# Attention keys in 16 KB runs and 2 MB loads, a gather moved between transposes, the store from ScalarE

## The chip, the cores and the metric

The kernel runs on one core of a Trainium2 chip. The metric is the device time of one execution in microseconds (us); lower is better. The core has TensorE (PE, its weight loads PEld), VectorE (DVE), ScalarE (ACT), GpSimd (POOL) and SyncE (SP), which work side by side and wait for each other through semaphores. Transfers between the device memory and the on-chip memory are issued by SP or ACT and are carried out by 16 DMA engines. TensorE writes its results to PSUM, from where VectorE and ScalarE read them.

## The reference

One decoding step: eight batches, one query token each. `x` is normalised, attention runs over the last 1,024 of 4,096 cached positions, with 32 query heads on 8 kv heads, and its result is multiplied by a gate from a small feed-forward net. All inputs are bf16.

```python
def A(x, k_cache, v_cache, wq, wo):          # x (8, 1, 512), caches (8, 8, 4096, 128)
    W = 1024
    q = (x @ wq).reshape(8, 1, 32, 128).transpose(0, 2, 1, 3)
    k = repeat(k_cache[:, :, -W:, :], 4, axis=1)
    v = repeat(v_cache[:, :, -W:, :], 4, axis=1)
    p = softmax(q @ k^T * 128 ** -0.5)
    return (p @ v).transpose(0, 2, 1, 3).reshape(8, 1, 4096) @ wo

def B(x, w_gate, w_up, w_down):
    return (gelu(x @ w_gate) * (x @ w_up)) @ w_down

xn = layernorm(x)
out = x + A(xn, ...) * silu(B(xn, ...))
```

The window of keys is 16.8 MB, that of values as much. wq and wo are 4.2 MB each, w_gate, w_up and w_down 1.8 MB each. (Below, MB in the sizes of loads stands for 1,024 x 1,024 bytes: a set is 1 MB.)

## The kernel before, in words

**Sets.** The attention is cut into 16 sets: set s is kv head s // 2 with batches 0 to 3 (s even) or 4 to 7 (s odd). `load_set` (L105) brings a set's keys or values as one DMA of 1 MB: partition 4p + g holds, for batch g of the set, the 32 positions 32p to 32p + 31, which lie together in the device memory, 8 KB. Rows of neighbouring batches lie 8 MB apart there. The tiles come from the pool `ring` with 9 buffers (L68), keys and values together. The weights come through `big` (L69), 5 buffers of 2 MB, used in turn: three loads of wq (1, 1 and 2 MB), w_gate, w_up, w_down, and two tiles for wo.

**One set's way.** All of it is done with four batches at once:

- `transpose_quarter` (L400), four times a set: four TensorE transposes of 128x128 f32 (two bf16 in each) by the identity `identf` into a PSUM tile `kT_ps` (four buffers), which VectorE (even quarter, L414) or ScalarE (odd, L416) copies into `kT` as 128x1024 bf16.
- `scores` (L420): eight matmuls with the queries (L425) into `sc`; VectorE adds the mask of the batches and takes each row's maximum (L433).
- `maxima` (L441): two f32 matmuls (L444) bring the row maxima together in `m_ps`; VectorE makes the bias of the exponential from them (L449).
- `exponentials` (L455): ScalarE's Exp with its sum (L458). `turn` (L466): VectorE transposes the result (L468).
- `value_half` (L474), twice: eight matmuls each with the values (L479); after the second, ScalarE copies the sum to `blk` (L486).
- `gather` (L490), once a head, for its two sets: eight matmuls (L496) into `m_ps`, the same PSUM tile that `maxima` uses; VectorE divides (L502 to L507) and turns the result into `oR` (L512).

**The order of work** is written out by hand, in steps t of half a set, and each engine works through its own list in that order:

```python
for t in range(2 * NS + LV + 3):          # NS = 16, LV = 5: t = 0 to 39
    s, i = divmod(t, 2)
    # i == 0: exponentials(s-2); fetch K(s)
    # transpose_quarter(s, 2*i), transpose_quarter(s, 2*i + 1); two hidden_steps
    # i == 0: turn(s-2), scores(s-1)
    # i == 1: gather((s-4)//2) for even s >= 4, then maxima(s-1)
    # value_half of set (t - 5) // 2; t = 6, 7: down(0), down(1); t = 8: fold(), gate()
```

So set s is transposed in steps 2s and 2s+1, scored in 2s+2, its maxima are taken in 2s+3, its exponentials in 2s+4, its values in 2s+5 and 2s+6. The last gather, that of head 7, is in step 37; nothing is left for the two steps behind it. `hidden_steps` are the eight operations of the feed-forward net's middle; `down`, `fold` and `gate` are its end.

**The queues.** SP issues every load, in the order in which the loop fetches: wq in three loads (L99), w_gate, w_up, K0, K1, K2, w_down, then V0, K3, V1, K4 and so on to V12, K15, V13, V14, V15, and last wo (L128) in eight pieces, 1 MB, five of 512 KB, 384 KB and 128 KB. A load waits for its buffer to be free, and every load behind it on SP waits too. ScalarE issues one load, x (L90). After the loop, 128 matmuls (L587) multiply `oR` by wo, VectorE applies the gate (L598) and adds x (L599), and SP stores the 8 KB result (L600).

Of the kernel before, what the change touches and what calls it, by code (L numbers as in the profile page):

```python
# [11 lines left out]
BF16 = mybir.dt.bfloat16  # L12
FP32 = mybir.dt.float32
# [4 lines left out]
def kernel(  # L18
# [13 lines left out]
    nc = tc.nc  # L32

    B, Sq, D = A_x.shape
    Hkv, Sk, Dh = A_k_cache.shape[1], A_k_cache.shape[2], A_k_cache.shape[3]
# [3 lines left out]
    win0 = Sk - W  # L39
# [4 lines left out]
    P = nc.NUM_PARTITIONS  # L44
# [2 lines left out]

    G = 4  # L50
    NB = B // G
    NS = Hkv * NB
    KP = P // G
    NCH = W // KP
    NC = G * rep
    SET = NCH * Dh
    QT = 4
    CP = NCH // 2
    QP = CP // QT
# [5 lines left out]


    lead = ctx.enter_context(tc.tile_pool(name="lead", bufs=1))
    ring = ctx.enter_context(tc.tile_pool(name="ring", bufs=9))  # L68
    big = ctx.enter_context(tc.tile_pool(name="big", bufs=5))  # L69
    kT_pool = ctx.enter_context(tc.tile_pool(name="kT_pool", bufs=2))  # L70
    p_pool = ctx.enter_context(tc.tile_pool(name="p_pool", bufs=2))
# [1 line left out]
    small = ctx.enter_context(tc.tile_pool(name="small", bufs=3))  # L73
# [31 lines left out]
    def load_set(cache, s):  # L105
        h, b0 = s // NB, (s % NB) * G
        t = slot()
        nc.sync.dma_start(
            out=t,
            in_=cache[b0 : b0 + G, h, win0:Sk, :].rearrange(  # L110
                "g (p c) d -> p g (c d)", p=KP
            ),
        )
        return t.rearrange("p (c d) -> p c d", c=NCH)

    HB = 2 * SET // (rep * D)
    wo_tiles = {}
# [279 lines left out]

    K, V, kT, sc, P_, pT, blk = {}, {}, {}, {}, {}, {}, {}

    def transpose_quarter(s, i):  # L400
        ps = ps_kT.tile([P, QP, P], FP32, name="kT_ps")
        for c in range(QP):
            nc.tensor.transpose(  # L403
                ps[:, c, :],
                K[s][:, 2 * (i * QP + c) : 2 * (i * QP + c) + 2, :]
                .rearrange("p c d -> p (c d)").bitcast(FP32),
                identf,
            )
        if i == 0:
            kT[s] = kT_pool.tile([P, CP, P, 2], BF16, name="kT")  # L410
        out = kT[s][:, i * QP : (i + 1) * QP].rearrange("p c k e -> p (c k e)")
        in_ = ps.rearrange("p c k -> p (c k)").bitcast(BF16)
        if i % 2 == 0:
            nc.vector.tensor_copy(out=out, in_=in_)  # L414
        else:
            nc.scalar.activation(out=out, in_=in_, func=ACT.Copy)  # L416

    top = {}

    def scores(s):  # L420
        ps = ps_sc.tile([P, CP, 32], FP32, name="sc")
        t = kT.pop(s)
        for e in range(2):
            for R in range(NR):
                nc.tensor.matmul(  # L425
                    ps[32 * R : 32 * R + 32],
                    qT[:, e, s].rearrange("p c b j -> p (c b j)"),
                    t[:, :, 32 * R : 32 * R + 32, e],
                    start=(e == 0), stop=(e == 1), skip_group_check=True,
                )  # L430
        sc[s] = small.tile([P, CP * 32], FP32, name="sc_sb", bufs=2)
        top[s] = small.tile([P, 1], FP32, name="top")
        nc.vector.tensor_tensor_reduce(  # L433
            out=sc[s], in0=ps.rearrange("p c k -> p (c k)"),
            in1=own.rearrange("p c b g -> p (c b g)"),
            op0=ALU.add, op1=ALU.max, scale=1.0, scalar=NEG, accum_out=top[s],
        )
# [3 lines left out]
    def maxima(s):  # L441

        ps = m_top
        nc.tensor.matmul(  # L444
            ps, top.pop(s).to_broadcast([P, P]), identf, start=True, stop=True
        )
        scr = small.tile([P, P], FP32, name="scr", bufs=1)
        bias = small.tile([P, 1], FP32, name="bias")
        nc.vector.tensor_tensor_reduce(  # L449
            out=scr, in0=ps, in1=same.rearrange("p x n -> p (x n)"),  # L450
            op0=ALU.add, op1=ALU.min, scale=-scale, scalar=-NEG, accum_out=bias,
        )
        biases[s] = bias

    def exponentials(s):  # L455
        blk[s] = small.tile([P, 2, Dh + 1], FP32, name="blk", bufs=4)
        P_[s] = p_pool.tile([P, CP * 32], BF16, name="p")
        nc.scalar.activation(  # L458
            out=P_[s], in_=sc.pop(s), func=ACT.Exp, scale=scale, bias=biases.pop(s),
            accum_out=blk[s][:, 0, Dh : Dh + 1],  # L460
        )
        nc.gpsimd.tensor_copy(  # L462
            out=blk[s][:, 1, Dh : Dh + 1], in_=blk[s][:, 0, Dh : Dh + 1]
        )

    def turn(s):  # L466
        pT[s] = p_pool.tile([P, CP, 32], BF16, name="pT")
        nc.vector.transpose(  # L468
            out=pT[s].rearrange("p c k -> p (c k)"), in_=P_.pop(s)
        )  # L470
# [3 lines left out]
    def value_half(s, i):  # L474
        if i == 0:
            o_ps[s] = ps_o.tile([P, 2, Dh], FP32, name="o_ps")
        for c in range(i * CP // 2, (i + 1) * CP // 2):
            q = c % NR
            nc.tensor.matmul(  # L479
                o_ps[s][32 * q : 32 * q + 32].rearrange("p c d -> p (c d)"),  # L480
                pT[s][:, c, :],
                V[s][:, 2 * c : 2 * c + 2, :].rearrange("p c d -> p (c d)"),
                start=(c < NR), stop=(c >= CP - NR), skip_group_check=True,
            )
        if i == 1:
            nc.scalar.activation(out=blk[s][:, :, 0:Dh], in_=o_ps.pop(s), func=ACT.Copy)  # L486
            pT.pop(s)
            V.pop(s)

    def gather(h):  # L490

        ps = m_out
        for b in range(NB):
            t = blk.pop(h * NB + b)
            for c in range(2):
                nc.tensor.matmul(  # L496
                    ps, sums[:, c, b].rearrange("p j b f -> p (j b f)"), t[:, c, :],
                    start=(b == 0 and c == 0), stop=(b == NB - 1 and c == 1),
                )

        rec = small.tile([P, 1], FP32, name="rec")
        nc.vector.tensor_scalar(  # L502
            out=rec, in0=ps[:, Dh : Dh + 1], scalar1=0.5, scalar2=None, op0=ALU.max
        )
        nc.vector.reciprocal(out=rec, in_=rec)
        o = small.tile([P, rep, Dh // rep], BF16, name="o")
        nc.vector.tensor_scalar(  # L507
            out=o, in0=ps[:, 0:Dh].rearrange("p (i r) -> p r i", r=rep),
            scalar1=rec, scalar2=None, op0=ALU.mult,
        )  # L510

        nc.vector.transpose(  # L512
            out=oR[:, h].rearrange("p r b -> p (r b)"),
            in_=o.rearrange("p r i -> p (r i)"),
        )


    AHEAD = 3
    down_tiles = []
    seq = []  # L520
    for s in range(AHEAD):
        seq.append(("K", s))
    seq.append(("D", 0))
    for s in range(NS):
        seq.append(("V", s))
        if s + AHEAD < NS:
            seq.append(("K", s + AHEAD))
    pending = list(seq)

    def fetch(kind, s):  # L530
        while True:
            k, i = pending.pop(0)
            if k == "K":
                K[i] = load_set(A_k_cache, i)
            elif k == "V":
                V[i] = load_set(A_v_cache, i)
            else:
                down_tiles.append(load_rows(B_w_down, 0, NFC, NFC, "wd"))
            if (k, i) == (kind, s):
                return  # L540


    LV = 2 * (AHEAD - 1) + 1
    for t in range(2 * NS + LV + 3):
        s, i = divmod(t, 2)
        if i == 0 and 0 <= s - 2 < NS:
            exponentials(s - 2)
        if s < NS:
            if i == 0:
                fetch("K", s)  # L550
            transpose_quarter(s, 2 * i)
            transpose_quarter(s, 2 * i + 1)
        for _ in range(2):
            if hidden_steps:
                hidden_steps.pop(0)()
        if i == 0 and 0 <= s - 2 < NS:
            turn(s - 2)
        if i == 0 and 0 <= s - 1 < NS:
            scores(s - 1)
        if i == 1 and s >= 4 and s % 2 == 0:  # L560
            gather((s - 4) // 2)
        if i == 1 and 0 <= s - 1 < NS:
            maxima(s - 1)
        s3, i3 = divmod(t - LV, 2)
        if 0 <= s3 < NS:
            if i3 == 0:
                fetch("V", s3)
            value_half(s3, i3)
        if t == 2 * AHEAD:
            down(0)  # L570
        if t == 2 * AHEAD + 1:
            down(1)
        if t == 2 * AHEAD + 2:
            fold()
            gate()

# [5 lines left out]
    for h0, r0, n, nh in pieces:  # L582
# [14 lines left out]
    o_flat = out.flatten_outer_dims()  # L597
    nc.vector.tensor_tensor(out=tmp, in0=s_ps, in1=g_sb, op=ALU.mult)  # L598
    nc.vector.tensor_tensor(out=out_sb, in0=tmp, in1=xf, op=ALU.add)  # L599
    nc.sync.dma_start(  # L600
        out=o_flat.rearrange("b (q c) -> q b c", q=NQB),
        in_=out_sb.rearrange("(i f) c -> f i c", f=PB)[0],
    )
# [30 lines left out]
```

## Time and profile before

| | before |
|---|---|
| median of 3 runs | 121.08 us (120.98 to 121.09) |
| the profiled execution | 120.90 us |
| its span in the trace | 119.1 us |
| PE busy, share of span | 83.7 us, 70% |
| DVE busy | 66.8 us, 56% |
| ACT busy | 54.8 us, 46% |
| K loads | 16 of 1,024 KB, 17.3 us from issue to landing |
| V loads | 16 of 1,024 KB, 19.0 us from issue to landing |
| wo loads | 5 of 512 KB, 15.5 us from issue to landing |

The span is the time from the first to the last event of the profiled execution; its own time is 1.8 us longer. The page cuts the span into 40 slices of 2.98 us and gives, for each, the clock that TensorE was granted (in tenths of full speed, 9 being 90% or more), the busy share of the DMA engines (in tenths), and what they moved in GB/s. The chain of work that ended last is followed back from the last instruction; a DMA in it means that the work behind it waited for a transfer. In the timeline, a line has start, duration, engine, kernel line and operation, and in brackets how long the engine had been idle and what ended that. A line of the windows view has the stretch, its length, the busy time of PE, PEld, DVE, ACT and POOL (with the number of their instructions), the granted clock, the DMA share and GB/s.

### The profile page before, as it was taken

How to read it: one execution, taken by the hardware profiler on the slowest of the kernel's cores; microseconds unless marked ns; L12 is line 12 of the kernel's file. 1: busy time of each engine (PE TensorE's matmuls, PEld its weight loads, DVE VectorE, ACT ScalarE, POOL GpSimd, SP SyncE). 2: the span in 40 equal slices, each digit the busy share in tenths (PEclk: the TensorE clock that was granted, in tenths of full speed). 3: DMA queues.
4: the chain of work that ended last, by engine and by line, in shares of the span. 5: the costliest groups of instructions: out<-in, count | busy, mean ns of one | idle time of the engine just before them, and what ended most of it. 6: DMA issues, size and time to landing. Idle time of an engine off the chain costs nothing.

```text
span 119.1 us, 2421 instructions
## 1 busy us (share of the span) xinstructions
PE 83.7 (70%) x974; PEld 57.6 (48%) x974; DVE 66.8 (56%) x187; ACT 54.8 (46%) x89; POOL 5.1 (4%) x24
## 2 busy tenths in 40 slices
PE   0250629599582897879979989976979679847740
PEld 0110216197451563647757657754755467525620
DVE  0600132957799456367767767766849477552300
ACT  4000030039808538538838838748547647722000
POOL 7000000000000000000000000000000000000000
PEclk9999999999999679999999999999999999996898
DMA  3999999999999999999999999999999999999930
GB/s 94 424 454 440 414 433 410 432 424 450 411 418 426 429 429 418 432 421 429 429 418 429 424 432 410 435 429 418 426 426 429 424 432 424 410 420 420 421 141 6
DMA packets 6815, 47.61 MB, mean 400 GB/s; under 512 B 780, under 2 KB 916, under 8 KB 1940
## 3 DMA queue, kind: packets, MB, share of 16 engines
q1 hardware_dynamic: 6788, 47.46, 95.0%
q8 instruction: 7, 0.11, 0.3%
q14 instruction: 4, 0.03, 0.1%
q10 hardware_dynamic: 16, 0.01, 0.1%
HBM read 47.46 MB, written 0.01 MB: 398 GB/s over the span
## 4 chain that ended last, share of the span: by engine, by line
DMA 71%; PE 22%; DVE 2%; ACT 2%; issue 1%; SPq 1%; ACTq 0%
DMA slot<-in_A_k_cache_dram 36%; DMA slot<-in_A_v_cache_dram 15%; PE kT_ps L403 11%; DMA big<-in_A_wo_dram 10%; DMA big<-in_A_wq_dram 9%; PE sc L425 3%; PE o_ps L479 3%; PE m_ps L496 2%; PE m_ps L444 1%; PE s L370 1%; ACT kT L416 1%; SPq L99 1%; DVE o L507 1%; PE s L587 0%; ACT f_sb L378 0%
## 5 line engine op out<-in xcount | busy, mean ns | idle before, releaser
L416 ACT ACTIVATE kT<-kT_ps 128x1024 bf16<-128x1024 bf16 x32 | 32.5, 1022 | 22.0 <-PE kT_ps L403 22.0
L403 PE MATMUL kT_ps<-identf,slot 128*128 128x128 f32 x256 | 37.5, 296 | 3.4 <-DMA slot<-in_A_k_cache_dram 3.3
L403 PEld LDWEIGHTS kT_ps<-identf,slot 128*128 128x128 f32 x256 | 30.3, 150 | 11.7 <-issue 3.9
L414 DVE COPY kT<-kT_ps 128x1024 bf16<-128x1024 bf16 x32 | 22.0, 688 | 12.8 <-PE kT_ps L403 12.8
L458 ACT ACTIVATE p<-sc_sb,bias 128x512 bf16<-128x512 f32 x16 | 11.5, 718 | 16.7 <-DVE bias L449 16.7
L444 PE MATMUL m_ps<-identf,top 128*128 128x128 f32 x32 | 7.3, 311 | 10.0 <-DVE o L507 5.8
L479 PE MATMUL o_ps<-slot,pT 128*32 128x256 bf16 x256 | 13.0, 287 | 1.5 <-DVE pT L468 1.5
L468 DVE STREAM_TRANSPOSE pT<-p 128x512 bf16<-128x512 bf16 x16 | 11.3, 704 | 2.4 <-ACT p L458 2.4
L433 DVE CUSTOM_DVE_ANT_0 sc_sb<-sc,own 128x512 f32<-128x512 f32 x16 | 10.5, 656 | 0.5 <-PE sc L425 0.5
L425 PE MATMUL sc<-kT,qT 128*32 128x512 bf16 x128 | 10.3, 400 | 0.5 <-ACT kT L416 0.5
L444 PEld LDWEIGHTS m_ps<-identf,top 128*128 128x128 f32 x32 | 4.7, 187 | 12.0 <-DVE o L507 7.2
L496 PE MATMUL m_ps<-blk,sums 128*128 128x129 f32 x64 | 9.8, 300 | 0.0
L496 PEld LDWEIGHTS m_ps<-blk,sums 128*128 128x128 f32 x64 | 8.7, 208 | 0.9 <-issue 0.6
L479 PEld LDWEIGHTS <-pT 128*32 128x32 bf16 x256 | 5.5, 98 | 7.2 <-DVE pT L468 1.8
L462 POOL COPY blk<-blk 128x1 f32<-128x1 f32 x16 | 3.0, 185 | 101.5 <-ACT p L458 101.5
L486 ACT ACTIVATE blk<-o_ps 128x256 f32<-128x256 f32 x16 | 6.1, 381 | 2.2 <-PE o_ps L479 2.2
L276 PE MATMUL sc<-big,xnT 128*32 128x512 bf16 x16 | 2.5, 611 | 5.5 <-DMA big<-in_A_wq_dram 5.2
L283 DVE CAST q_row<-sc 128x512 bf16<-128x512 f32 x2 | 1.3, 686 | 8.6 <-PE sc L276 8.6
L287 ACT ACTIVATE q_row<-o_ps 128x512 bf16<-128x512 f32 x2 | 1.1, 595 | 10.5 <-PE o_ps L276 10.5
L449 DVE CUSTOM_DVE_ANT_0 scr<-m_ps,same 128x128 f32<-128x128 f32 x16 | 4.6, 289 | 1.6 <-PE m_ps L444 1.6
L502 DVE TENSOR_SCALAR rec<-m_ps 128x1 f32<-128x1 f32 x8 | 1.3, 158 | 7.0 <-PE m_ps L496 6.9
L276 PEld LDWEIGHTS <-xnT 128*32 128x32 bf16 x32 | 1.1, 120 | 7.6 <-issue 7.2
(69 smaller groups left out, 54.2 us busy)
## 6 DMA issues: line engine op xcount, KB each, us to landing
slot<-in_A_k_cache_dram SPq DMA_DIRECT2D x16, 1024.0 KB, 17.3
slot<-in_A_v_cache_dram SPq DMA_DIRECT2D x16, 1024.0 KB, 19.0
big<-in_A_wo_dram SPq DMA_DIRECT2D x5, 512.0 KB, 15.5
big<-in_A_wq_dram SPq DMA_DIRECT2D x2, 1024.0 KB, 5.8
big<-in_A_wq_dram SPq DMA_DIRECT2D x1, 2048.0 KB, 11.2
big<-in_B_w_gate_dram SPq DMA_DIRECT2D x1, 1792.0 KB, 14.8
big<-in_B_w_up_dram SPq DMA_DIRECT2D x1, 1792.0 KB, 18.5
big<-in_B_w_down_dram SPq DMA_DIRECT2D x1, 1792.0 KB, 27.7
```

What stands on the lines that cost most here:

```text
L403: nc.tensor.transpose(ps[:, c, :], K[s][:, 2 * (i * QP + c) : 2 * (i * QP + c) + 2, :] .rearrange("p c d -> p (c d)").bitcast(FP32), identf,)
L414: nc.vector.tensor_copy(out=out, in_=in_)
L416: nc.scalar.activation(out=out, in_=in_, func=ACT.Copy)
L425: nc.tensor.matmul(ps[32 * R : 32 * R + 32], qT[:, e, s].rearrange("p c b j -> p (c b j)"), t[:, :, 32 * R : 32 * R + 32, e], start=(e == ...
L433: nc.vector.tensor_tensor_reduce(out=sc[s], in0=ps.rearrange("p c k -> p (c k)"), in1=own.rearrange("p c b g -> p (c b g)"), op0=ALU.add, ...
L444: nc.tensor.matmul(ps, top.pop(s).to_broadcast([P, P]), identf, start=True, stop=True)
L449: nc.vector.tensor_tensor_reduce(out=scr, in0=ps, in1=same.rearrange("p x n -> p (x n)"), op0=ALU.add, op1=ALU.min, scale=-scale, scalar=- ...
L458: nc.scalar.activation(out=P_[s], in_=sc.pop(s), func=ACT.Exp, scale=scale, bias=biases.pop(s), accum_out=blk[s][:, 0, Dh : Dh + 1],)
L468: nc.vector.transpose(out=pT[s].rearrange("p c k -> p (c k)"), in_=P_.pop(s))
L479: nc.tensor.matmul(o_ps[s][32 * q : 32 * q + 32].rearrange("p c d -> p (c d)"), pT[s][:, c, :], V[s][:, 2 * c : 2 * c + 2, :].rearrange("p ...
L486: nc.scalar.activation(out=blk[s][:, :, 0:Dh], in_=o_ps.pop(s), func=ACT.Copy)
L496: nc.tensor.matmul(ps, sums[:, c, b].rearrange("p j b f -> p (j b f)"), t[:, c, :], start=(b == 0 and c == 0), stop=(b == NB - 1 and c == 1),)
```

## The change

Keys are loaded for a whole kv head at a time. `load_pair` brings the keys of all eight batches as one DMA of 2 MB, into a buffer of `big`: partition 8p' + b holds, for batch b, the 64 positions from 64p' on, 16 KB that lie together. Values stay as they are, in sets of 1 MB, in the `ring`, which has 5 buffers instead of 9.

`transpose_part` takes the place of `transpose_quarter`: eight parts a head, each of four transposes into one PSUM tile. TensorE's output is written in another order than its columns come: partition 8p' + 4h + g with half x of its positions becomes set h, column (2p' + x)4 + g, which is the order that the values have. In memory, the columns go to PSUM in groups of four. `kT` holds both sets of a head (two blocks), still in two buffers; a part's copy writes 512 elements of each block. The number of transposes (256) and copies (64) stays.

The loop has the same half-set steps: head m is transposed in steps 4m to 4m+3; set s is scored in step 2s+4, its maxima are in 2s+5, its exponentials and turn in 2s+6, its values in 2s+7 and 2s+8. Head h's gather is in step 4h+11, between the step's two transposing parts; the last one is in step 39. `blk` has 6 buffers instead of 4. SP's order is now wq, w_gate, w_up, K0, K1, w_down, V0, and then K(m), V(2m-3), V(2m-2) for m from 2 to 7, then V13, V14, V15 and wo. The store of the result is issued by ScalarE.

```diff
--- before.py
+++ after.py
@@ -65,7 +67,7 @@
 
 
     lead = ctx.enter_context(tc.tile_pool(name="lead", bufs=1))
-    ring = ctx.enter_context(tc.tile_pool(name="ring", bufs=9))
+    ring = ctx.enter_context(tc.tile_pool(name="ring", bufs=5))
     big = ctx.enter_context(tc.tile_pool(name="big", bufs=5))
     kT_pool = ctx.enter_context(tc.tile_pool(name="kT_pool", bufs=2))
     p_pool = ctx.enter_context(tc.tile_pool(name="p_pool", bufs=2))
@@ -112,6 +114,15 @@
             ),
         )
         return t.rearrange("p (c d) -> p c d", c=NCH)
+
+    def load_pair(cache, h):
+
+        t = big.tile([P, 2 * SET], BF16, name="big")
+        nc.sync.dma_start(
+            out=t,
+            in_=cache[:, h, win0:Sk, :].rearrange("b (p c) d -> p b (c d)", p=KP // 2),
+        )
+        return t.rearrange("p (c d) -> p c d", c=2 * NCH)
 
     HB = 2 * SET // (rep * D)
     wo_tiles = {}
@@ -397,19 +408,22 @@
 
     K, V, kT, sc, P_, pT, blk = {}, {}, {}, {}, {}, {}, {}
 
-    def transpose_quarter(s, i):
-        ps = ps_kT.tile([P, QP, P], FP32, name="kT_ps")
-        for c in range(QP):
-            nc.tensor.transpose(
-                ps[:, c, :],
-                K[s][:, 2 * (i * QP + c) : 2 * (i * QP + c) + 2, :]
-                .rearrange("p c d -> p (c d)").bitcast(FP32),
-                identf,
-            )
+    def transpose_part(m, i):
+
+
+        ps = ps_kT.tile([P, 2, 2, KP // 2, 2, G], FP32, name="kT_ps")
+        for c in range(2):
+            for x in range(2):
+                k0 = x * NCH + 2 * (2 * i + c)
+                nc.tensor.transpose(
+                    ps[:, :, c, :, x, :].rearrange("p h b g -> p b h g"),
+                    K[m][:, k0 : k0 + 2, :].rearrange("p c d -> p (c d)").bitcast(FP32),
+                    identf.rearrange("p (b h g) -> p b h g", h=2, g=G),
+                )
         if i == 0:
-            kT[s] = kT_pool.tile([P, CP, P, 2], BF16, name="kT")
-        out = kT[s][:, i * QP : (i + 1) * QP].rearrange("p c k e -> p (c k e)")
-        in_ = ps.rearrange("p c k -> p (c k)").bitcast(BF16)
+            kT[m] = kT_pool.tile([P, 2, CP, P, 2], BF16, name="kT")
+        out = kT[m][:, :, 2 * i : 2 * i + 2].rearrange("p h c k e -> p h (c k e)")
+        in_ = ps.rearrange("p h c b x g -> p h (c b x g)").bitcast(BF16)
         if i % 2 == 0:
             nc.vector.tensor_copy(out=out, in_=in_)
         else:
@@ -417,9 +431,9 @@
 
     top = {}
 
-    def scores(s):
+    def scores(s, m, y):
         ps = ps_sc.tile([P, CP, 32], FP32, name="sc")
-        t = kT.pop(s)
+        t = kT[m][:, y]
         for e in range(2):
             for R in range(NR):
                 nc.tensor.matmul(
@@ -453,7 +467,7 @@
         biases[s] = bias
 
     def exponentials(s):
-        blk[s] = small.tile([P, 2, Dh + 1], FP32, name="blk", bufs=4)
+        blk[s] = small.tile([P, 2, Dh + 1], FP32, name="blk", bufs=6)
         P_[s] = p_pool.tile([P, CP * 32], BF16, name="p")
         nc.scalar.activation(
             out=P_[s], in_=sc.pop(s), func=ACT.Exp, scale=scale, bias=biases.pop(s),
@@ -515,23 +529,18 @@
         )
 
 
-    AHEAD = 3
+    NK = NS // 2
     down_tiles = []
-    seq = []
-    for s in range(AHEAD):
-        seq.append(("K", s))
-    seq.append(("D", 0))
-    for s in range(NS):
-        seq.append(("V", s))
-        if s + AHEAD < NS:
-            seq.append(("K", s + AHEAD))
-    pending = list(seq)
+    pending = [("K", 0), ("K", 1), ("D", 0), ("V", 0)]
+    for m in range(2, NK):
+        pending += [("K", m), ("V", 2 * m - 3), ("V", 2 * m - 2)]
+    pending += [("V", u) for u in range(2 * NK - 3, NS)]
 
     def fetch(kind, s):
         while True:
             k, i = pending.pop(0)
             if k == "K":
-                K[i] = load_set(A_k_cache, i)
+                K[i] = load_pair(A_k_cache, i)
             elif k == "V":
                 V[i] = load_set(A_v_cache, i)
             else:
@@ -540,37 +549,45 @@
                 return
 
 
-    LV = 2 * (AHEAD - 1) + 1
-    for t in range(2 * NS + LV + 3):
-        s, i = divmod(t, 2)
-        if i == 0 and 0 <= s - 2 < NS:
-            exponentials(s - 2)
-        if s < NS:
+
+    def due(t, d):
+        s, r = divmod(t - d, 2)
+        return s if r == 0 and 0 <= s < NS else None
+
+    for t in range(2 * NS + 8):
+        m, i = divmod(t, 4)
+        s = due(t, 6)
+        if s is not None:
+            exponentials(s)
+        if m < NK:
             if i == 0:
-                fetch("K", s)
-            transpose_quarter(s, 2 * i)
-            transpose_quarter(s, 2 * i + 1)
+                fetch("K", m)
+            transpose_part(m, 2 * i)
+        if t >= 11 and t % 4 == 3:
+            gather((t - 11) // 4)
+        if m < NK:
+            transpose_part(m, 2 * i + 1)
         for _ in range(2):
             if hidden_steps:
                 hidden_steps.pop(0)()
-        if i == 0 and 0 <= s - 2 < NS:
-            turn(s - 2)
-        if i == 0 and 0 <= s - 1 < NS:
-            scores(s - 1)
-        if i == 1 and s >= 4 and s % 2 == 0:
-            gather((s - 4) // 2)
-        if i == 1 and 0 <= s - 1 < NS:
-            maxima(s - 1)
-        s3, i3 = divmod(t - LV, 2)
-        if 0 <= s3 < NS:
+        if s is not None:
+            turn(s)
+        s = due(t, 4)
+        if s is not None:
+            scores(s, s // 2, s % 2)
+        s = due(t, 5)
+        if s is not None:
+            maxima(s)
+        u, i3 = divmod(t - 7, 2)
+        if 0 <= u < NS:
             if i3 == 0:
-                fetch("V", s3)
-            value_half(s3, i3)
-        if t == 2 * AHEAD:
+                fetch("V", u)
+            value_half(u, i3)
+        if t == 8:
             down(0)
-        if t == 2 * AHEAD + 1:
+        if t == 9:
             down(1)
-        if t == 2 * AHEAD + 2:
+        if t == 10:
             fold()
             gate()
 
@@ -597,7 +614,7 @@
     o_flat = out.flatten_outer_dims()
     nc.vector.tensor_tensor(out=tmp, in0=s_ps, in1=g_sb, op=ALU.mult)
     nc.vector.tensor_tensor(out=out_sb, in0=tmp, in1=xf, op=ALU.add)
-    nc.sync.dma_start(
+    nc.scalar.dma_start(
         out=o_flat.rearrange("b (q c) -> q b c", q=NQB),
         in_=out_sb.rearrange("(i f) c -> f i c", f=PB)[0],
     )
```

## The prediction, made before the changed kernel ran

> **What bounds the kernel now.** I read four views, in this order: the page's slices, the chain of work that ended last, TensorE's timeline over the last 25 us, and the sync engine's DMA issues. First the page:
>
> ```profile
> PEclk9999999999999679999999999999999999996898
> DMA  3999999999999999999999999999999999999930
> GB/s 94 424 454 440 414 433 410 432 424 450 411 418 426 429 429 418 432 421 429 429 418 429 424 432 410 435 429 418 426 426 429 424 432 424 410 420 420 421 141 6
> DMA packets 6815, 47.61 MB, mean 400 GB/s; under 512 B 780, under 2 KB 916, under 8 KB 1940
> q1 hardware_dynamic: 6788, 47.46, 95.0%
> ```
>
> The 16 DMA engines are full from the second slice to the last but one, on one queue. No engine's work is the limit: it is the time that 47.46 MB take in packets. The chain ends so:
>
> ```profile
> 103.18 11.99 DMA big<-in_A_wo_dram
> 115.16 0.04 issue
> 115.20 0.59 PE s L587 x16
> 115.80 0.02 issue
> 115.82 0.30 DVE tmp L598
> 116.13 0.02 issue
> 116.15 0.29 DVE out_sb L599
> ```
>
> The last piece of wo lands at 115.16; sixteen matmuls, two VectorE operations and the store follow. Whatever makes the queue's total shorter moves 115.16 earlier, as long as the attention of the last head is done by then. How near it is, TensorE's timeline tells:
>
> ```profile
> 93.23 1.09 PE L403 MATMUL kT_ps<-identf,slot 128*128 128x128 f32 x8 [1.12 <-DMA slot<-in_A_k_cache_dram]
> ...
> 97.84 0.49 PE L444 MATMUL m_ps<-identf,top 128*128 128x128 f32 x2 [0.83 <-DVE o L507]
> ...
> 108.01 1.05 PE L479 MATMUL o_ps<-slot,pT 128*32 128x256 bf16 x16 [1.51 <-DVE pT L468]
> 108.99 2.09 PE L496 MATMUL m_ps<-blk,sums 128*128 128x129 f32 x8
> 111.01 1.38 PE L587 MATMUL s<-big,oR 128*32 128x128 bf16 x80
> ```
>
> K14 lands at 93.2, step t=28 begins, and the last gather ends at 111.0, some 4 us before the end. From 52 to 98 us, two sets take 9.9 us (83.28 to 93.23), of which TensorE waits 1.1 us for keys and 0.83 us after a gather: DMA sets the pace, TensorE has little to spare.
>
> **The change, part by part.**
>
> *Keys in 16 KB runs.* The trace keeps every DMA packet with its size and duration. Medians by size: 4 KB 159 ns, 8 KB 309 ns, 16 KB (the third load of wq, 2 MB) 611 ns, and 9 ns for the 4-byte write with which each engine reports a DMA as done. Check: 8,192 B in 309 ns on 16 engines are 424 GB/s, the rate of the slices. The keys are 16.8 MB: 2,048 packets of 8 KB, 128 on each engine; they become 64 of 16 KB. Saving: 64 x (2 x 309 - 611) = 64 x 7 ns = **0.45 us**. Ends: nothing, if time goes by bytes alone; 64 x 9 ns = 0.58 us by the step from 4 to 8 KB (2 x 159 - 309). I take 7 ns, the row with this very size. Eight K loads fewer are eight reports fewer on each engine: 8 x 9 ns = **0.07 us**. Nothing hides this; engines that are always busy end by so much earlier.
>
> [...]
>
> *Do the loads still keep the queue full?* The ring shrinks from 9 to 5 slots, for values alone; K pairs use the five 2 MB buffers of `big`. On SP's list:
>
> ```profile
> 6.66 0.33 SPq L99 DMA_DIRECT2D big<-in_B_w_down_dram  x1
> 7.96 0.54 SPq L108 DMA_DIRECT2D slot<-in_A_v_cache_dram  x1
> 12.83 0.54 SPq L108 DMA_DIRECT2D slot<-in_A_k_cache_dram  x1
> ```
>
> w_down waits at 6.66 for wq's first buffer, the next two each for a landing: eight loads are out at a time. After the change K0 stands where w_down stood (6.66), K1 waits for wq's second buffer (its matmuls end at 9.0), w_down for the third (14.7); behind them on SP wait all V loads. At 14.7 gate, up, K0 and K1 (7.5 MB, over 17 us at 2.45 us a MB) are still out or moving, so no gap. Later V(u) waits for the end of step 2u-2 and is used from step 2u+7; when K(m) lands, V(2m-3), V(2m-2), K(m+1), V(2m-1), V(2m), K(m+2) are issued: 8 MB, 19 us of cover. Only if steps fell 15 us or more behind would the queue run dry. Cost nothing. K(m) ends at the same place in the byte order as K14 or any even set before (36.25 MB for K7), so step 4m can begin when it did.
>
> *Transposes.* 256 as before, 64 copies of 128x1024 as before (VectorE 688, ScalarE 1,022 ns). New: TensorE writes its 128 columns to PSUM in runs of 4, and a copy writes two blocks. No row shows such a write. Ends: nothing, and twice the time for transposes (at half clock, 39.20, eight took 1.64 instead of 1.03 us); for copies twice too (the strided 128x512 cast of L283 took 686 ns, as long as 1,024 contiguous elements). I take nothing: the copies stay contiguous over 512 elements, and each column is still one write per partition. If it costs, it is the fifth rival.
>
> *Gather between two parts.* Now each gather is followed by the maxima in the same PSUM tile, which wait 0.83 us for VectorE's L507. Eight transposes move between: four of them take 0.51 us (eight in 1.03), so about 0.5 of the 0.83 goes, seven times. It's TensorE time under the DMA: worth nothing at the end, except that steps keep up better: 8.3 instead of 8.8 us for four steps against 9.9 us of transfers.
>
> *Two steps more.* Exponentials come at 2s+6 instead of 2s+4, values at 2u+7 instead of 2u+5, so the loop ends with step 39, not 37. During the run that is latency under the queue; at the end it is not obviously free (second rival).
>
> *Store by ScalarE.* The two rows:
>
> ```profile
> 0.73 0.58 ACTq L90 DMA_DIRECT2D x_sb<-in_A_x_dram  x1
> ...
> 116.47 0.69 SPq L600 DMA_DIRECT2D out_dram<-out_sb  x1
> ```
>
> An issue of 0.58 against 0.69 gives -0.1. The other end is +1.0: x landed 1.7 us after its issue's end, the store 0.7; but x ran beside wq at full load, and the store runs alone. I take **-0.1**. ScalarE has nothing behind it.
>
> Sum: -0.45 - 0.07 - 0.1 = -0.62 us. The profiled execution took 120.90 us (span 119.1, 1.8 around it), 0.18 below the median; it would become 120.3, and the median 121.08 **120.5**.
>
> **The rivals.**
>
> *Second: the tail takes over, slower.* Count from K7's landing (93.2 before, minus the saving). The last wo lands 21.9 later and its 16 matmuls end at 22.5. Steps 28 to 31 end at 8.3 (kT copy too). From there one chain, by the rows from 98 to 111 us: scores(14) to 8.8; VectorE does turn(13) first, then the row maxima, to 10.8; maxima(14) 11.25, bias 11.6, exponentials 12.55, turn 13.3, row maxima(15) 14.0, the VectorE end of gather(6) 14.8, maxima(15) 15.25, bias 15.65, exponentials 16.6, turn 17.3. V15 and the last gather took 3.0 us before (108.01 to 111.0), at half clock:
>
> ```profile
> 107.00:108.00 1.00, 0.00 (x0) 0.00 (x0) 0.71 (x1) 0.49 (x3) 0.18 (x1) 0.91 1.05 430
> 108.00:109.00 1.00, 0.99 (x17) 0.47 (x17) 0.00 (x0) 0.00 (x0) 0.00 (x0) 0.50 1.03 422
> ```
>
> So the gather ends at 20.3, or at 18.7 with full clock (0.62 and 1.06 us for the same groups). Behind it wait 112 output matmuls (80 in 1.38, so 1.9 us), to 22.2, and the last 16. That is a tie with the DMA at one slow stretch (3.4 us at 0.50, from 107.5), 1.6 us of room without, and 1.5 us late with a second one, which falls on gather(6), the maxima and the scores (+1.0, +0.2, +0.3). It decides once the last gather ends over 20.3 us after K7. Price 0.6 to 1.5 us over the forecast: **121.1 to 121.9, say 121.6**. For it: TensorE is busy only half of that tail. Against: the same half before (104 to 107.5: 1.66 of 3.5) gave one slow stretch, not two.
>
> [...]
>
> *Third: the packets save nothing,* and the time stays: 121.08 - 0.1 = **121.0**. For it: windows with 14 and 16 KB packets (4 to 24 us) show 430, those with 8 KB (50 to 103) 425 GB/s, a small difference between neighbouring slices that scatter from 410 to 454. Against: the packet medians, hardly scattering.
>
> *Fourth: eight rows 8 MB apart.* One load now walks 8 batches instead of 4, neighbours 8 MB apart, and engines could meet in the same part of the memory. The slowest 16 KB packet took 1,018 ns; if all did, 64 x 407 ns = 26 us, **147**. Against: the 8 KB rows, 4 batches at the same 8 MB, hold 309 ns.
>
> [...]
>
> *Fifth: the scattered PSUM write is slow.* At the half-clock duration, 32 transposes a pair cost 2.5 us more; 8.3 + 2.5 = 10.8 us against 9.9: 0.9 a pair over seven pairs, and 2.5 in the tail: some **128**. Nothing in the rows speaks for it.
>
> **How the numbers follow.** Chances: forecast 0.53, tail 0.25, no saving 0.13, memory 0.03, PSUM 0.06. What this kernel's measurement can tell from no change is about 0.2%, 0.24 us: faster means below 120.84. Faster: 0.53, and 0.05 of the tail's mildest and best store cases, 0.58. Same, 120.84 to 121.32: the third rival and a mild tail, 0.12 + 0.08 = 0.20. Slower: the rest of the tail and the last two, 0.22. Range: down to 120.0 (the profiled execution's 120.28, with 0.58 for the packets and another 0.15 in the store), up through the tail to 121.9; what lies outside is the last two rivals and a little of the tail.
>
> **What would show it.** Right: some 1,024 packets fewer, 16 KB ones at 611 ns, the DMA row full to the end, the last wo landing near 114.6, TensorE still waiting for it, store issue near 0.6. Wrong: a last gather over 20.3 us behind K7 and no wait before the last L587 (tail); 16 KB packets above 618 ns (third, fourth); eight transposes over 1.03 us (fifth); a gap in the DMA row, which would mean that the smaller ring starves the queue.

## The result and the profile after

The changed kernel took 172.16 us in the median against 121.01; the ratio is 1.406 (95% interval 1.400 to 1.411), some 49 us more. The forecast was 120.5 us. (Executions disturbed from outside, of this kernel and of some experiments, are left out of the ratios, so a median can lie above its ratio.) The profiled execution took 170.71 us, its span is 168.9. These are the page's lines that answer to those shown of before; a slice is 4.22 us here:

```profile
PEclk9999995589579557996995697599759975997558
DMA  5999999999999999999999999999899999999800
GB/s 192 435 430 431 439 225 210 225 210 276 412 287 206 215 411 227 192 287 367 206 217 324 293 221 206 382 213 225 198 398 204 208 235 413 433 407 419 361 33 2
DMA packets 5662, 47.61 MB, mean 282 GB/s; under 512 B 652, under 2 KB 788, under 8 KB 1812
q1 hardware_dynamic: 5600, 47.45, 94.4%
```

The DMA row is as full as before, and the bytes are the same. But where the keys move, the rate is 192 to 235 GB/s in most slices instead of 425; the weights at the start (430 and more) and wo at the end (407 to 433) have kept theirs. A full row says that the engines hold work, not that it advances. TensorE now waits for keys, 43.3 us in all where it waited 3.3 before; here in its list of waits (total us, times, longest):

```profile
PE kT_ps L418 <- DMA big<-in_A_k_cache_dram: 43.3, 7, 8.9
```

By the trace's packet records, the 16 KB packets of the keys take 1,254 ns in the median, those of wq, in the same execution, 611. Values are touched too: of all 8 KB packets 27% take over 330 ns, the mean is 372 instead of 312. On each engine that makes 64 x 1,201 (the mean) - 128 x 312 = 37 us for the keys and 144 x 60 ns = 8.7 us for the other 8 KB packets, 46 of the 49.8 us between the two spans. Another 3.1 us come after the transfers: by the traces' semaphore records the last piece of wo landed at 115.5 us before and at 162.2 now, and TensorE's last matmul ended 0.3 us behind it before (115.8) and 3.4 us now (165.6). That is the tail:

```profile
140.37 1.97 PE L418 MATMUL kT_ps<-identf,big 128*128 128x128 f32 x8 [6.81 <-DMA big<-in_A_k_cache_dram]
...
145.42 1.09 PE L418 MATMUL kT_ps<-identf,big 128*128 128x128 f32 x8
146.44 0.62 PE L439 MATMUL sc<-kT,qT 128*32 128x512 bf16 x8
...
160.77 2.09 PE L510 MATMUL m_ps<-blk,sums 128*128 128x129 f32 x8
162.79 2.78 PE L604 MATMUL s<-big,oR 128*32 128x128 bf16 x128
```

The last keys landed at 140.3, the last gather ended at 162.8, and then all 128 output matmuls ran in one piece: they waited for no wo. The lines from 145.42 to 146.44 also show the transposes with the scattered PSUM write, at a granted clock of 1.00: eight in 1.02 us, as before. (The first line's 1.97 us for eight fall in a stretch with a clock of 0.50, from 140.3 to 143.7.)

### The profile page after: what moved, and what is told of

Same layout as the page of the kernel before. It is cut to its first block, busy times and chain, and to the rows that moved or that the text cites. A ratio compares the mean times of both kernels' runs of the same rounds, so it can differ in the third digit from the quotient of the medians.

```text
span 168.9 us, 2390 instructions
## 1 busy us (share of the span) xinstructions
PE 95.8 (57%) x974; PEld 66.7 (39%) x974; DVE 68.1 (40%) x187; ACT 55.0 (33%) x89; POOL 5.1 (3%) x24
## 4 chain that ended last, share of the span: by engine, by line
DMA 68%; PE 21%; DVE 5%; ACT 3%; issue 1%; ACTq 0%
DMA big<-in_A_k_cache_dram 65%; PE kT_ps L418 10%; PE m_ps L510 3%; DMA big<-in_A_wq_dram 3%; PE sc L439 3%; PE o_ps L493 2%; PE s L604 2%; PE m_ps L458 1%; DVE h_row L361 1%; ACT p L472 1%; DVE pT L482 1%; ACT L354 1%; ACT kT L430 1%; DVE o L521 0%; DVE hT L366 0%
## 5 line engine op out<-in xcount | busy, mean ns | idle before, releaser
L418 PE MATMUL kT_ps<-identf,big 128*128 128x128 f32 x256 | 46.5, 337 | 48.7 <-DMA big<-in_A_k_cache_dram 43.3
L418 PEld LDWEIGHTS kT_ps<-identf,big 128*128 128x128 f32 x256 | 37.3, 175 | 58.0 <-DMA big<-in_A_k_cache_dram 27.5
L430 ACT ACTIVATE kT<-kT_ps 128x1024 bf16<-128x1024 bf16 x32 | 32.6, 1022 | 81.5 <-PE kT_ps L418 81.5
L493 PE MATMUL o_ps<-slot,pT 128*32 128x256 bf16 x256 | 14.6, 317 | 1.1 <-DVE pT L482 1.1
L439 PE MATMUL sc<-kT,qT 128*32 128x512 bf16 x128 | 12.9, 487 | 0.0
L510 PE MATMUL m_ps<-blk,sums 128*128 128x129 f32 x64 | 10.5, 316 | 0.5 <-DVE g_sb L406 0.5
L510 PEld LDWEIGHTS m_ps<-blk,sums 128*128 128x128 f32 x64 | 9.3, 223 | 1.3 <-DVE g_sb L406 0.7
L493 PEld LDWEIGHTS <-pT 128*32 128x32 bf16 x256 | 6.1, 108 | 8.8 <-issue 3.5
L458 PEld LDWEIGHTS m_ps<-identf,top 128*128 128x128 f32 x32 | 5.5, 216 | 7.0 <-DVE o L521 4.9
L316 DVE COPY qT<-kT_ps 64x128 bf16<-64x128 bf16 x8 | 2.3, 288 | 4.1 <-PE kT_ps L309 4.0
```

What stands on the lines that cost most here:

```text
L418: nc.tensor.transpose(ps[:, :, c, :, x, :].rearrange("p h b g -> p b h g"), K[m][:, k0 : k0 + 2, :].rearrange("p c d -> p (c d)").bitcast( ...
L439: nc.tensor.matmul(ps[32 * R : 32 * R + 32], qT[:, e, s].rearrange("p c b j -> p (c b j)"), t[:, :, 32 * R : 32 * R + 32, e], start=(e == ...
L458: nc.tensor.matmul(ps, top.pop(s).to_broadcast([P, P]), identf, start=True, stop=True)
L493: nc.tensor.matmul(o_ps[s][32 * q : 32 * q + 32].rearrange("p c d -> p (c d)"), pT[s][:, c, :], V[s][:, 2 * c : 2 * c + 2, :].rearrange("p ...
L510: nc.tensor.matmul(ps, sums[:, c, b].rearrange("p j b f -> p (j b f)"), t[:, c, :], start=(b == 0 and c == 0), stop=(b == NB - 1 and c == 1),)
```

## The experiments

**First question: is it the load's pattern, and what in it?** A kernel of loads alone, with these stages, 4.2 MB each (`rows(cache, h, nb, b0, pos, p)` reads `cache[b0:b0+nb, h, -pos:]` as "b (p c) d -> p b (c d)"; S1 is 8 KB a partition, S2 16 KB):

```diff
+    stage([(P, S1, rows(C, h, 4, b0, 1024, 32)) for h in range(2) for b0 in (0, 4)])
+    stage([(P, S2, rows(C, h, 8, 0, 1024, 16)) for h in range(2)])
+    stage([(P, S1, rows(C, h, 8, 0, 512, 16)) for h in range(4)])
+    stage([(P, S2, rows(C, h, 4, 0, 2048, 32)) for h in range(2)])
+    stage([(P, S2, rows(C, h, 2, 0, 4096, 64)) for h in range(2)])
...
+    stage([(64, S2, rows(C, h, 4, b0, 1024, 16)) for h in range(2) for b0 in (0, 4)])
...
```

> Loads alone, nothing computed: this kernel leaves out the whole attention and the net and stores x, so only its transfers are read. Twelve stages one after the other, each of 4 MB from the caches, each begun when the one before has landed: (1) 4 batches, 8 KB pieces, as before; (2) 8 batches, 16 KB, as in the changed kernel; (3) 8 batches, 8 KB pieces that lie together; (4) 4 batches, 16 KB, 128 partitions; (5) 2 batches, 16 KB; (6) one contiguous stretch, 16 KB pieces; (7) 4 batches, 16 KB, two loads of 64 partitions; (8) 8 batches, 8 KB, every second piece; (9) 8 batches, 4 KB pieces; (10) as 2 and (11) as 1 from the values' cache; (12) as 2 with the batch as the outer order of the partitions. Theory A, number of batches: what is slow is one load that walks eight batches 8 MB apart. Then 2, 3, 8, 9 and 10 run at 205 to 230 GB/s and 1, 4, 5, 6, 7 and 11 at 420 or more. Theory B, size of the piece: 16 KB pieces of the cache are slow. Then 2, 4, 5, 6, 7 and 10 run at about 210 and 1, 3, 8, 9 and 11 at 420. Theory C, the load collides with what the engines do on chip at the same time: then all stages run at 420, stage 2 too. Stage 12 is to tell whether another order of the same pieces over the DMA engines helps: under A, if the engines that run side by side take different batches, no better than 210.

The windows view of its stages 1 to 12, one line each, cut inside each stage; the last two numbers are the DMA share and GB/s:

```profile
3.00:12.00 9.00, 0.00 (x0) 1.00 1.01 424
15.00:33.00 18.00, 0.00 (x0) 1.00 1.02 218
37.00:54.00 17.00, 0.00 (x0) 1.00 1.01 219
58.00:67.00 9.00, 0.00 (x0) 1.00 1.02 433
70.00:79.00 9.00, 0.00 (x0) 1.00 1.00 426
82.00:92.00 10.00, 0.00 (x0) 1.00 0.94 393
96.00:114.00 18.00, 0.00 (x0) 1.00 0.98 204
118.00:134.00 16.00, 0.00 (x0) 1.00 1.01 224
138.00:154.00 16.00, 0.00 (x0) 1.00 1.03 234
159.00:177.00 18.00, 0.00 (x0) 1.00 0.96 204
180.00:189.00 9.00, 0.00 (x0) 1.00 1.00 420
194.00:229.00 35.00, 0.00 (x0) 1.00 0.49 113
```

Stage 2 is slow by itself (218 GB/s), so theory C falls. Stages 4, 5 and 6 move 16 KB rows at full rate (433, 426 and 393), and stages 3, 8 and 9 are slow with 8 and 4 KB (219, 224 and 234): theory B falls. Theory A holds for all stages but the seventh: four batches, and yet 204 GB/s, where stage 4 moves four batches at 433. But stage 7 differs in a second thing, it writes to 64 partitions only. What 2, 3, 7, 8, 9 and 10 share is 16 groups of rows (204 to 234 GB/s); the fast ones have 32, 64 or 128 (393 to 433). In stage 12 the DMA share is 0.49: by the packet records 7.8 packets are under way at once in the mean, against 16.1 in stage 2, as if 8 of the 16 engines carried it, and at 113 GB/s these would run at half rate too (14 GB/s each, where stage 4 has 27).

Two experiments in the full kernel say the same. The first splits the load by batches:

```diff
-            out=t,
-            in_=cache[:, h, win0:Sk, :].rearrange("b (p c) d -> p b (c d)", p=KP // 2),
+                out=t[64 * y : 64 * y + 64, :],
+                in_=cache[y * G : (y + 1) * G, h, win0:Sk, :].rearrange(
+                    "g (p c) d -> p g (c d)", p=KP // 2
+                ),
```

> The changed kernel with each 2 MB load of keys split into two of 1 MB, one for four batches each, on 64 partitions each; pieces stay 16 KB, buffers, order and all work stay. Theory A (eight batches in one load): key packets back near 611 ns, the DMA at 420 GB/s, and then the end is set by the tail of the changed order: 22.4 us from the last keys' landing to the end of the last gather in the changed kernel, against 21.9 us to the last piece of wo; some 121 to 123 us. Theory B (16 KB pieces): still 165 to 185 us.

It took 168.4 us (one execution): four batches in a load, on 64 partitions, don't help. The second splits it by positions:

```diff
-            out=t,
-            in_=cache[:, h, win0:Sk, :].rearrange("b (p c) d -> p b (c d)", p=KP // 2),
+                out=t[:, x * SET : (x + 1) * SET],
+                in_=cache[:, h, win0:Sk, :].rearrange(
+                    "b (p x c) d -> x p b (c d)", p=KP // 2, x=2
+                )[x],
```

> The changed kernel with each 2 MB load of keys split into two of 1 MB by positions: eight batches, 8 KB pieces, every second piece of the cache each; all else stays. Theory A: 8 KB packets of the keys at 500 to 620 ns instead of 309, 160 to 185 us. Theory B: 309 ns, 121 to 123 us.

169.04 us, ratio 1.394 (1.387 to 1.401): 8 KB rows are as slow. So theory B falls here as well. Theory A failed in the first, as it was put; but that run's loads, like stage 7's, write to 64 partitions each, and the next experiment shows that this can be slow by itself (205 GB/s on partitions 0 to 63). What rules A out is that experiment's stage 3, which is slow with a single batch (231).

**Second question: the memory's side or the chip's?** What is left are two theories. Theory E, put in the expectation below, has the cause in the rows that are read; the other has it in the partitions that are written and in how the load is grouped over them. Loads alone can part them: the same source, written 32 partitions further on.

```diff
+    stage([(P, S1, near(b, 16, 8, 32, 9)) for b in range(4)])
+    stage([(P, S1, near(b, 32, 4, 32, 5)) for b in range(4)])
+    stage([(64, S2, rows(C, h, 4, b0, 1024, 16)) for h in range(2) for b0 in (0, 4)])
+    stage([((32, 96), S2, rows(C, h, 4, b0, 1024, 16)) for h in range(2) for b0 in (0, 4)])
+    stage([((64, 128), S2, rows(C, h, 4, b0, 1024, 16)) for h in range(2) for b0 in (0, 4)])
+    stage([(64, S2, flat[b][0:4096, :].rearrange("(p c) d -> p (c d)", p=64)) for b in range(4)])
+    stage([((32, 96), S2, flat[b][0:4096, :].rearrange("(p c) d -> p (c d)", p=64)) for b in range(4)])
```

(`near` reads p groups of n rows from one stretch, with a row left out behind each group; `flat[b]` is a batch's cache as one list of positions.)

> Loads alone again (attention and net are left out, x is stored), eleven stages of 4 MB, the tenth of 8. (1) the pattern before; (2) the changed kernel's; (3) 16 groups of 8 rows of 8 KB, all within 1.2 MB of one batch, so no row is far from another; (4) the same with 32 groups of 4 rows; (5) 4 batches, 16 KB, on partitions 0 to 63; (6) the same on partitions 32 to 95; (7) the same on 64 to 127; (8) one contiguous stretch, 16 KB rows, on partitions 0 to 63; (9) the same on 32 to 95; (10) four batches to partitions 0 to 63 from SP and four to 64 to 127 from ACT at the same time; (11) the pattern before. [...] Theory E, the source: 16 groups of rows 16 KB apart, read side by side, meet in the device memory. Then 5, 6 and 7 are alike at about 212, and 3, 4, 8 and 9 at 370 or more. [...]

The windows of its stages 3 to 9:

```profile
37.00:54.00 17.00, 0.00 (x0) 1.00 1.02 231
58.00:67.00 9.00, 0.00 (x0) 1.00 1.00 421
71.00:89.00 18.00, 0.00 (x0) 1.00 1.01 205
93.00:102.00 9.00, 0.00 (x0) 1.00 0.98 415
106.00:124.00 18.00, 0.00 (x0) 1.00 0.99 204
126.00:144.00 18.00, 0.00 (x0) 1.00 1.00 204
148.00:157.00 9.00, 0.00 (x0) 1.00 0.99 422
```

Theory E falls: it has stages 5, 6 and 7 alike, and 3 and 8 at 370 GB/s or more. Partitions 32 to 95 take four batches in 16 groups at 415 GB/s, partitions 0 to 63 the same rows at 205 and 64 to 127 at 204. A contiguous source goes at 204 to partitions 0 to 63 and at 422 to 32 to 95. Rows of one small stretch of one batch, in 16 groups of 8, go at 231, in 32 groups of 4 at 421. In these stages, where the rows come from has next to no part in it (205 and 204 to partitions 0 to 63, 415 and 422 to 32 to 95); where they go, and in what groups, decides. Stage 10, two queues at once, one to partitions 0 to 63 and one to 64 to 127, moved 225.

Why these partitions and this grouping take half the rate is not shown. No record has which engine wrote which partition, or what engines that write at the same time share on the way. The records have the time of a packet: 1,254 ns for 16 KB of the keys in the changed kernel, 611 for 16 KB of wq, which is 13 and 27 GB/s an engine. That the engines hold each other up on the writing side is the author's inference, from stages 5 to 9, from stages 3 and 4, which differ mainly in the grouping (231 and 421), and from stage 12 of the first kernel of loads, where an outer order of eight has a DMA share of 0.49.

**Third question: what does the rest of the change cost?** The changed kernel with the rows of before, everything else as changed:

```diff
-            out=t,
-            in_=cache[:, h, win0:Sk, :].rearrange("b (p c) d -> p b (c d)", p=KP // 2),
+                out=t[:, y * SET : (y + 1) * SET],
+                in_=cache[y * G : (y + 1) * G, h, win0:Sk, :].rearrange(
+                    "g (p c) d -> p g (c d)", p=KP
+                ),
...
-                    ps[:, :, c, :, x, :].rearrange("p h b g -> p b h g"),
+                    ps[:, x, c].rearrange("p b x g -> p (b x g)"),
...
-                    identf.rearrange("p (b h g) -> p b h g", h=2, g=G),
+                    identf,
```

> The changed kernel with the rows of before: each head's keys come as two loads of 1 MB, four batches in 8 KB pieces on 128 partitions, into the halves of the same 2 MB buffer, and the transposes write plain columns; buffers, order of loads, parts, gather, the two steps more and the store by ScalarE stay as changed. All theories: key packets at 309 ns and the DMA full. What is left is the rest of the change. By my second rival the last gather ends 20.3 us (22.4 as in the changed kernel's trace) after the last keys' landing, against 21.9 to the last piece of wo: with the store (0.5 us) 121.5 to 123.7. If the tail is hidden: 121.3 to 121.5.

121.61 us, ratio 1.0038 (1.0022 to 1.0055): without the new rows the 49 us are gone. Its DMA row is full (shares of 0.98 to 1.02 from 90.0 to 110.8 us, 0.92 in the next 3.4 us beside the last pieces of wo), so the smaller ring starves nothing. Its timeline:

```profile
93.34 0.98 PE L421 MATMUL kT_ps<-identf,big 128*128 128x128 f32 x7 [1.18 <-DMA big<-in_A_k_cache_dram]
...
111.27 2.09 PE L513 MATMUL m_ps<-blk,sums 128*128 128x129 f32 x8
113.29 3.30 PE L607 MATMUL s<-big,oR 128*32 128x128 bf16 x128
```

The last gather ends at 113.36, 20.1 us behind the last keys (93.3). The 128 output matmuls then take 3.3 us and wait for nothing: TensorE, not the DMA, sets the end, at 116.6 instead of 115.8. Two windows from 107.4 on show why they are slow; the granted clock is the third number from the right:

```profile
107.40:110.80 3.40, 1.54 (x30) 1.04 (x34) 1.61 (x5) 1.08 (x3) 0.18 (x1) 0.78 1.02 419
110.80:114.20 3.40, 3.40 (x56) 2.76 (x52) 0.69 (x4) 0.39 (x1) 0.00 (x0) 0.50 0.92 368
```

The store alone, in the kernel before:

```diff
-    nc.sync.dma_start(
+    nc.scalar.dma_start(
         out=o_flat.rearrange("b (q c) -> q b c", q=NQB),
```

> The kernel before with one edit, the store of the result issued by ScalarE. By the prediction's term 0.1 us faster, 120.9; the other end was 1 us slower. In the changed kernel's trace the issue took 0.64 us against 0.69, so I expect no difference that can be measured.

121.34 us, ratio 1.0039 (1.0026 to 1.0051): slower by 0.47 us. The issue is indeed shorter (0.64 against 0.69 us). SP's wait for the store at the program's end, first before, then here, seems to say that the store takes longer:

```profile
SPq L629 <- DMA out_dram<-out_sb: 0.7, 1, 0.7
```

```profile
SPq L629 <- DMA out_dram<-out_sb: 1.7, 1, 1.7
```

But the two waits begin at different places: before, SP issues the store itself and begins to wait at 117.5; here it waits from 116.5 on. The traces' semaphore records give the landing itself: 118.26 before, with the issue's start at 116.47, and 118.19 here, with the issue's start at 116.40. Both are 1.79 us; the store lands no later from ScalarE, and its shorter issue makes it land no sooner. The lost time lies behind the landing: from there to the trace's last event it is 0.87 us before and 1.32 here, and most of the difference is between the first two of the DRAIN instructions with which SP closes the program, whose starts lie 0.07 us apart before and 0.43 here. The pause doesn't come with the queue: the trace of the run above, also with the store by ScalarE, has 0.84 us behind the landing, that of the run below, with SP, 0.85. What makes it in this one kernel is not shown.

Both put right, rows and store:

```diff
-    nc.scalar.dma_start(
+    nc.sync.dma_start(
         out=o_flat.rearrange("b (q c) -> q b c", q=NQB),
```

> As the run before it, with the store issued by SP. 0.4 to 0.5 us below that one, as ScalarE's store cost 0.5 us when it was the only edit; if the tail is hidden 120.8 to 121.0, if not 121.0 to 123.2.

121.54 us, ratio 1.0027 (1.0008 to 1.0046). Its times fall into two groups, five from 120.86 to 120.98 and four from 121.54 to 121.73, so what the store costs here can't be read from the medians, 121.61 with ScalarE and 121.54 with SP. The times with ScalarE fall into the same two groups, three from 120.97 to 121.17 and six from 121.57 to 121.89; group against group, by their means, ScalarE's store costs 0.15 us in the short one and 0.02 in the long one. Two groups are what a tail on the edge gives, with a slow clock in it or without, and the granted clock of the executions says the same: its mean is 0.91 to 0.93 in all ten of the long groups and 0.94 to 1.00 in all eight of the short ones. To test it, 48 output matmuls were put where TensorE waits anyway:

```diff
             if i3 == 0:
                 fetch("V", u)
+            if t == 2 * NS + 5:
+                out_loads()
+                out_piece()
+                out_piece()
             value_half(u, i3)
```

(`out_loads` issues the eight wo loads, `out_piece` does the matmuls of one piece; those not done here follow after the loop. The condition stands inside `i3 == 0`.)

> The changed order with the rows of before and the store by SP, and one more edit: all wo loads are fetched right behind V15, and the 48 output matmuls of heads 0 to 2 stand before V15's matmuls, where TensorE waited 1.5 us. If the 0.9 us by which this order ended later (TensorE's last matmul at 116.5 instead of 115.8) is the tail, with 128 output matmuls at half clock behind the last gather, then 48 of them fewer there (1.2 us at half clock) let the DMA set the end again: 120.8 to 121.0 in all runs, where the version without it scattered between 120.9 and 121.7. If the tail isn't the cause, 121.5 as before.

120.98 us, ratio 1.0005 (0.9996 to 1.0014), all eleven from 120.79 to 121.21. The 0.7 us are gone, with mean clocks from 0.93 to 0.97, and TensorE waits for wo again:

```profile
112.01 1.27 PE L513 MATMUL m_ps<-blk,sums 128*128 128x129 f32 x8
113.22 0.85 PE L570 MATMUL s<-big,oR 128*32 128x128 bf16 x48
114.24 0.41 PE L570 MATMUL s<-big,oR 128*32 128x128 bf16 x16 [0.18 <-DMA big<-in_A_wo_dram]
115.13 0.58 PE L570 MATMUL s<-big,oR 128*32 128x128 bf16 x16 [0.48 <-DMA big<-in_A_wo_dram]
```

In this profiled execution the stretch at half clock came earlier, from 104.0 to 107.4 (0.50), and the clock was 1.00 from 107.4 to 116. So the run shows that the tail cost the 0.7 us, but doesn't part the time of the 48 matmuls from the clock in which the rest of them run.

**Fourth question: were the 0.45 us for larger packets real?** Loads alone, long stages, in the grouping that runs at full rate:

```diff
+    for _ in range(2):
+        long(S1, [rows(C, h, 4, b0, 1024, 32) for h in range(8) for b0 in (0, 4)])
+        long(S2, [rows(C, h, 4, 0, 2048, 32) for h in range(8)])
```

> Loads alone (attention and net are left out, x is stored): 16.8 MB in 16 loads of 1 MB with 8 KB rows, then 16.8 MB in 8 loads of 2 MB with 16 KB rows, both of four batches on 128 partitions, and both once more. It measures the term that the prediction took from packet durations alone. If 16 KB rows save 7 ns each and a load fewer 9 ns, the second and fourth stage end 0.5 us sooner than the first and third, of some 40 us; if time goes by bytes, they take the same.

From the first packet's start to the last one's end the stages (418 to 420 GB/s) took 40.21, 39.99, 40.42 and 39.88 us: 0.38 us less with 16 KB rows in the mean of two pairs, 0.22 and 0.54.

## Why the prediction was wrong, step by step

- **The step that failed** is the price of a key packet, "I take 7 ns, the row with this very size". The row was right for its size and its source, but wq's load writes 128 rows to 128 partitions, and the change writes 16 groups of 8. The time of a packet was taken as a property of its bytes; here it went with the grouping over the partitions too, 611 ns in wq's load and 1,254 in the keys'. With the right grouping the term holds (0.38 us measured, in two pairs that scatter from 0.22 to 0.54; 0.52 forecast with the reports); with this one it is some +46 us, 37 in the keys' own packets and 8.7 in the 8 KB packets, those of the values above all, that ran beside them.
- **"Nothing hides this; engines that are always busy end by so much earlier"** was right, and worked the other way.
- **The fourth rival** had the sign, and its price, made from the slowest 16 KB packet (1,018 ns), came to 26 us. That packet was none of the kernel's loads: it belongs to the instruction queue (q8 on the page); all 128 of wq's took 611 ns. Its mechanism was wrong: not distance in the device memory, as rows 8 MB apart run at 433 GB/s in 32 groups and rows of one stretch at 231 in 16. Its chance of 0.03 was argued from the packets of before, which have the same distance but another grouping.
- **That the loads keep the queue full** was right: no gap in the DMA row, neither in the changed kernel (0.8 or more in every slice between the first and the last two) nor with the rows of before (0.98 to 1.02 from 90.0 to 110.8 us).
- **Second rival, the tail**: its mechanism is shown, with the rows of before. There the last gather, forecast 20.3 us behind the last keys, came at 20.1 (in the changed kernel at 22.5, with two stretches at half clock); what was too small is the output matmuls behind it, 2.2 us forecast and 3.3 at half clock. It cost 0.7 us in ten executions of eighteen; by that, an estimate, it would have taken as much as the forecast gain in about half of the executions even if the rows had kept their rate. The landing that the prediction counts to, 115.16, is that of the last wo piece but one; the last landed at 115.49. What starts a stretch at half clock is not shown: before, one came at 107.5, behind 3.5 us in which TensorE was busy for 1.66, and none behind 7.0 to 13.0, where it was busy for 1.19 of 6.0 us (the clock was 1.00 from 13.0 to 17.5).
- **Store by ScalarE**: -0.1 us forecast, nothing gained. The term took the issue's length for the price, but the store landed 1.79 us behind its issue's start from either queue. The other end, +1.0, rested on a misreading: the 0.7 us given for the store is SP's wait, which began 0.37 us behind the issue's end; the landing came 1.1 us behind it. As the only edit the store by ScalarE measured +0.47 us, none of it before the landing; in the changed order 0.02 to 0.15.
- **Transposes and copies**: taken at nothing, and they cost nothing: eight transposes 1.02 us, copies 689 and 1,022 ns against 688 and 1,022. The fifth rival falls.
- **Gather between two parts**: 0.5 of the 0.83 us were to go; TensorE's wait fell to 0.40, and four steps take 8.2 us with the rows of before (93.3 to 101.5), forecast 8.3.

Left open: the order in which an engine takes its rows, which no record shows, and whether another layout could bring 16 KB rows of this window at full rate; with 1,024 positions and eight batches, 128 partitions hold 16 groups of 8 and no more, and it wasn't tried further. No version tried beats the kernel before.

## What to carry to other kernels

Before a load is given another shape, ask on the writing side too: into how many groups does its outermost dimension cut the partitions (on 128 partitions 16 groups ran at 204 to 234 GB/s here, 32 or more at 393 to 433), and which partitions does it write (205 on 0 to 63, 415 on 32 to 95)? Carry a packet's duration over only from a load with the same grouping: 16 KB took 611 ns in wq's load and 1,254 in the keys'. The length of a wait isn't that of the transfer (waits of 0.7 and 1.7 us for stores that both landed 1.79 us behind their issue's start): ask where the wait began. And a DMA row at full share says nothing of the rate (a share of 1.02 at 218 GB/s and at 433): read GB/s next to it.

## What the runs showed of the hardware that was not expected

- Loads of 64 partitions run at half rate on partitions 0 to 63 (205 GB/s) and 64 to 127 (204), and at full rate on 32 to 95 (415).
- A load to 128 partitions in 16 outer groups of 8 runs at 204 to 234 GB/s with rows of 4, 8 and 16 KB, with 32 groups or more at 393 to 433 with rows of 8 and 16 KB.
- With the batch as the outer order of eight, the DMA share is 0.49 and the rate 113 GB/s, as if half of the engines worked, each at half rate.
- An 8 KB store at the end of the program lands 1.79 us behind its issue's start, from ScalarE's queue as from SP's. As the only edit, ScalarE's store made the kernel 0.47 us (0.31 to 0.62) slower, in the trace mostly by a pause behind the landing, whose cause is open.
